# The last 256 tokens of a fused attention and feed-forward kernel: all 48 output products with tokens as stationary operand

## The chip, the cores and the metric

The kernel runs on one core of one Trainium2 chip. Its time is the device time of one execution in microseconds (us); the median of three runs before the change is 250.54 us. A second number is used below: the span of one profiled execution, from its first to its last instruction. All clock times such as "at 246.59" are us from the start of that span. The engines are called as the profile calls them: PE is the matrix engine (TensorE) and PEld its weight loads, DVE the vector engine, ACT the scalar engine, POOL the general engine, SP the engine that only issues transfers. A "q" behind an engine's name (SPq, ACTq) marks its sequencer, which waits, branches and issues transfers.

## The reference

The reference first computes a linear attention with sketched features for 4 batches of 4 heads and 1088 positions of 32 numbers. That gives x, 4352 tokens of 128 features. A feed-forward layer with a rational activation then follows:

```
h = x @ w_in                      # 4352 x 2048
P = a[0] + a[1]*h + a[2]*h*h + a[3]*h*h*h
Q = 1.0 + abs(b[0])*abs(h) + abs(b[1])*h*h
g = P / (Q + 1e-06)
out = g @ w_out                   # 4352 x 128
```

The change is in the last product, `g @ w_out`, and only for the last 256 of the 4352 tokens.

## The kernel before, in words

The kernel never forms g. With 1/Q called r, it writes g @ w_out as a sum of three products: of r, of s = h*r, and of a third array g = (h*s or h*p, times p or s), each with its own copy of w_out that has been scaled by a coefficient of P (`w_sb`, three tiles in bf16). So one block of 128 hidden features costs three matmuls, one for each of r, s and g.

The feed-forward part is cut into units of 4096 columns, where a column is one token of one block of 128 hidden features. The first unit holds 256 tokens times all 16 blocks, fourteen units hold 512 tokens times 8 blocks, and the last two, units 15 and 16, hold 256 tokens times 16 blocks. For each unit the steps are: `h` (PE, the hidden products in float32), `e` (ACT, out of PSUM into bf16), `u` (DVE, absolute value), `ln`, `ex`, `ra` (ACT, three activations that give r; `rd` is DVE's form of the third), `s`, `m`, `v`, `x` (DVE products), `pa` or `pd` (p on ACT or DVE), `G` (PE, the output products) and `st` (the store). Units other than the last take each step in halves or whole; unit 16 takes its first half whole and its second half in two quarters (`QUARTER`), so that its end is fine-grained.

The order of all steps is written out by hand in the string `ORDER` (lines 27 to 61). Each step issues its instructions on its engine's queue, and every engine works its queue in that order. Waits between engines follow from the data. Nothing is rescheduled.

For unit 16 the output products come in nine parts, `G0:16` to `G8:16` (`terms`, lines 696 to 703). Parts 0, 1, 2 are r, s, g of the first eight blocks, parts 3, 4, 5 those of the next four, parts 6, 7, 8 those of the last four: 16 blocks times three arrays are 48 products. In queue order at the end of the program they stand as G0, then 24 products of unit 15, then G7, G4, G1, G3, G6, G2, G5, G8 of unit 16.

There are two forms of such a product.

- In the usual form (`gather`, lines 744 to 749) the weights are stationary and up to 512 tokens stream past. For unit 16 it is one load of 128x128 weights and one matmul of 256 columns. The sum `outs[t0]` in PSUM has the output features on its partitions and the tokens along its columns.
- In the swapped form (`by_token`, lines 708 to 718) the data is stationary, 128 tokens of one block at a time, and the 128 output features of the weights stream past. It is two loads of 128x128 and two matmuls of 128 columns for each product. There are two sums in PSUM, one for each 128 tokens, which already have tokens on partitions and features along columns, as the output has them in DRAM.

Before the change `LATE_PARTS = (5, 8)` says that parts 5 and 8, the last eight products, are swapped. The other 40 are in the usual form. The two kinds of sum are joined by two steps. `se` (`partial`, lines 725 to 728) copies the finished sum of the 40 products, 128x256 float32, out of PSUM into an `out_sb` tile on ACT. `sx` (`turned`, lines 730 to 734) turns each 128 columns of it with a matmul against the identity and adds them into the two swapped sums; it is the last work of PE. Then `st:16` (`store`, lines 755 to 761) copies the first swapped sum out of PSUM on ACT and the second on DVE, and each engine's copy is sent to DRAM by one transfer of 64 KB, the first issued by ACT, the second by SP.

The step `fl`, just ahead of `st:16`, loads a flag into a register of every engine (line 894). The flag says whether a second, general version of the whole kernel has to run (line 942); with these inputs it has not, and each engine branches past it at the end. On SP's queue the flag's load stands between the four transfers of `st:15` (line 771, the store of unit 15) and the last transfer (line 760).

Buffers: `bank()` gives one of four PSUM banks (pool `att`), a bank is given out again when its last reader is done; `out_sb` has two buffers.

Of the kernel before, what the change touches and what calls it, by code (L numbers as in the profile page):

```python
# [11 lines left out]
FP = mybir.dt.float32  # L12
# [7 lines left out]
class Fast:  # L20
# [35 lines left out]
u1:15 ra0:15 G1:12 G2:12 h1:16 G3:13 h0:16 ln1:15 e1:16 ex1:15 e0:16 s1:14 ra1:15 pd1:14 m1:14 st:12 u0:16 x1:14 h3:16  # L56
G3:14 G1:13 ln0:16 s1:15 e3:16 ex0:16 G5:13 h2:16 G1:14 G2:13 G0:14 e2:16 pd1:15 u3:16 ra0:16 G1:15 G5:14 G3:15 G2:14
G4:14 G0:15 G0:16 m1:15 u2:16 ln3:16 x1:15 ln2:16 ex3:16 ex2:16 ra3:16 s0:16 st:14 ra2:16 pa0:16 m0:16 pa2:16 G5:15
G2:15 G4:15 s3:16 s2:16 G7:16 hi:0 G4:16 G1:16 G3:16 pa3:16 m3:16 G6:16 m2:16 x0:16 G2:16 st:15 se:16 x2:16 G5:16
x3:16 G8:16 sx:16 fl:0 st:16  # L60
    """.split()
    W_ENG = (1, 1, 0, 0, 0, 1)
    P_ON_ACT = (0, 0, 0, 0, 0, 0, 0, 0, 0, 0, 0, 0, 0, 0, 0, 0, 0, 0, 0, 0, 0, 0, 0, 0, 0, 0, 0, 0, 0, 0, 0, 0, 1, 1)
# [10 lines left out]
class General:  # L74
# [37 lines left out]
    y2:16 G3:13 pd0:15 e0:16 G4:13 s0:15 e1:16 G5:13 y3:16 pa1:14 G0:15 u0:16 m0:15 G1:15 ln1:15 G0:14 m1:14 G1:14 w0:16  # L112
    G2:14 ex1:15 x0:15 G3:14 y0:16 G2:15 v1:14 G3:15 ln0:16 s1:15 x1:14 ex0:16 pd1:15 G5:14 m1:15 G0:16 ln2:16 s0:16 G4:15
    pa0:16 x1:15 G1:16 ex2:16 m0:16 G5:15 ln3:16 s2:16 x0:16 ex3:16 m2:16 G2:16 pa2:16 st:15 s3:16 G3:16 pa3:16 G4:16
    st:14 x2:16 m3:16 G6:16 G7:16 se:16 G5:16 x3:16 sx:16 G8:16 st:16
    """.split()
    W_ENG = (1, 1, 0, 0, 0, 1)
    P_ON_ACT = (1, 1, 0, 1, 1, 0, 1, 1, 0, 1, 1, 1, 1, 0, 1, 0, 1, 0, 1, 1, 0, 1, 0, 1, 1, 1, 0, 0, 1, 1, 0, 0, 1, 1)
# [10 lines left out]
def run(  # L129
# [13 lines left out]
    nc = tc.nc  # L143
# [24 lines left out]
    mid = ctx.enter_context(tc.tile_pool(name="mid", bufs=2))  # L168
# [31 lines left out]
    for i, s_in in enumerate((S1, S2)):  # L200
# [5 lines left out]
                      in_=bass.AP(tensor=k.tensor, offset=k.offset, ap=[[S * D // 32, 128], [W, NM], [1, 4 * D]]))  # L206
    nc.sync.dma_start(out=k0[:, 0:km].rearrange("p (m x) -> p m x", m=NM - 1)[:, :, 4 * D:],
                        in_=k0_src[:, 0:km].rearrange("p (m x) -> p m x", m=NM - 1)[:, :, 4 * D:])
# [19 lines left out]
    def turn(i, cols=512):  # L228
        idle_ps = bank()
        for _ in range(plan.TURNS[i]):  # L230
            nc.tensor.matmul(idle_ps[:, :cols], lhsT=idle[:, 0:128], rhs=idle[:, :cols], start=True, stop=True)
# [17 lines left out]
    ident = consts.tile([128, 128], FP, name="ident")  # L249
# [48 lines left out]
    def bank():  # L298
        return att.tile([128, 512], FP, name="att_ps")
# [217 lines left out]
    TC = 512  # L517
    units = []
# [7 lines left out]
    live = [dict() for _ in range(NU)]  # L526
    outs, summed = {}, {}
# [64 lines left out]
    def horner(i, h):  # L592
        return 2 * i + (h > 0) in plan.HORNER

    def squared(i, h):
        return 2 * i + (h > 0) in plan.SQ
# [99 lines left out]
    def terms(i):  # L696

        per = units[i][3]
        cuts = [(0, per // 2), (per // 2, per)]
        if i in plan.QUARTER:  # L700
            cuts[1:] = [(per // 2, 3 * per // 4), (3 * per // 4, per)]
        return [[(x, y, key) for x in range(*c)] if y != 1 or not (horner(i, n) or squared(i, n)) else []
                for n, c in enumerate(cuts) for y, key in enumerate(("r", "s", "g"))]

    LATE_PARTS = (5, 8)
    by_tok = []

    def by_token(i, part):
        t0, tl, f0, per = units[i]
        tokens(i)  # L710
        count = tl // 128
        for n in range(count):
            bk, done = by_tok[n]
            for x, y, key in terms(i)[part]:
                h, c = 2 * x // per, x % (per // 2) * tl + n * 128
                nc.tensor.matmul(bk[:, :128], lhsT=part_of(i, key, h)[:, c:c + 128], rhs=w_sb[y][:, f0 + x, :],
                                 start=done[0] == 0, stop=done[0] == done[1] - 1)
                done[0] += 1

    def tokens(i):  # L720
        if not by_tok:
            total = 1 + sum(len(terms(i)[n]) for n in LATE_PARTS)
            by_tok.extend((bank(), [0, total]) for _ in range(units[i][1] // 128))

    def partial(i):
        t0, tl = units[i][:2]
        live[i]["part"] = mid.tile([128, TC], FP, name="out_sb")
        nc.scalar.copy(out=live[i]["part"][:, :tl], in_=outs[t0][:, :tl])

    def turned(i):  # L730
        tokens(i)
        for n, (bk, done) in enumerate(by_tok):
            nc.tensor.matmul(bk[:, :128], lhsT=live[i]["part"][:, n * 128:(n + 1) * 128], rhs=ident, start=done[0] == 0, stop=done[0] == done[1] - 1)
            done[0] += 1

    def gather(i, part):
        t0, tl, f0, per = units[i]
        if t0 not in outs:
            outs[t0] = bank()
            summed[t0] = [0, sum(len(z) for j in range(NU) if units[j][0] == t0 for n, z in enumerate(terms(j)) if j < NU - 1 or n not in LATE_PARTS)]  # L740
        if i == NU - 1 and part in LATE_PARTS:
            by_token(i, part)
# [40 lines left out]
    def w_part(x):  # L783
        y, f = x // 2, x % 2 * (nf // 2)
        o, t = w_sb[y][:, f:f + nf // 2], w_out_sb_f[:, f:f + nf // 2]
        if fast:
            if plan.W_ENG[x]:
                nc.scalar.activation(out=o, in_=t, func=ACT.Copy, scale=a_k[:, y:y + 1])
            else:
                nc.vector.tensor_scalar(out=o, in0=t, scalar1=a_k[:, y:y + 1], scalar2=None, op0=AX.mult)  # L790
        elif y == 2:
            (nc.scalar.copy if plan.W_ENG[x] else nc.vector.tensor_copy)(out=o, in_=t)
        elif plan.W_ENG[x]:
            nc.scalar.activation(out=o, in_=t, func=ACT.Copy, scale=a_sb[:, y:y + 1])
        else:
            nc.vector.tensor_scalar(out=o, in0=t, scalar1=a_sb[:, y:y + 1], scalar2=None, op0=AX.mult)
# [37 lines left out]
    def fitting():  # L834
        g = nc.gpsimd
        aa1, aa2, aa3 = (a_abs[:, x:x + 1] for x in (1, 2, 3))
        g.tensor_mul(out=sq, in0=ab0, in1=ab0)
        by(lim, ab1, AX.mult, 2.0 ** -10)
        by(fit, ab1, AX.is_ge, 2.0 ** -20)
        by(b4, ab1, AX.mult, 2.0)  # L840
        by(fit, ab1, AX.is_le, 2.0 ** 20, AX.mult, fit)
        by(fit, ab0, AX.is_ge, lim, AX.mult, fit)
        by(fit, b4, AX.is_ge, sq, AX.mult, fit)
        by(lim, fit, AX.mult, -1.0, AX.add, 1.0)
        by(b_fit, b_abs, AX.mult, fit, AX.add, lim)
        by(b4, b_fit[:, 1:2], AX.mult, 4.0)
        g.tensor_mul(out=sq, in0=b_fit[:, 0:1], in1=b_fit[:, 0:1])
        by(c_fit[:, 1:2], b4, AX.mult, 1.0 + 1e-6, AX.subtract, sq)
        g.tensor_copy(out=c_fit[:, 0:1], in_=b_fit[:, 0:1])
        if plan.SQ:  # L850
            for x in (2, 3):
                by(c_fit[:, x:x + 1], a_sb[:, x:x + 1], AX.is_equal, 0.0, AX.add, a_sb[:, x:x + 1])
        else:
            g.tensor_copy(out=special, in_=lim)
# [49 lines left out]
    for step in plan.ORDER:  # L904
        name, i = step.split(":")
        i = int(i)
        if name in q_does:
            getattr(blocks[i](), q_does[name])()
        elif name in k_does:
            getattr(keys[i](), k_does[name][0])(*k_does[name][1:])  # L910
        elif name == "wo":
            w_part(i)
        elif name in loads:
            fetched[name, i] = loads[name](i)
        elif name == "tn":
            turn(i)
        elif name == "ba":
            nc.scalar.activation(out=b_abs, in_=b_sb, func=ACT.Abs)
            if fast:
                if plan.SQ:  # L920
                    nc.scalar.activation(out=a_abs, in_=a_sb, func=ACT.Abs)
                fitting()
            else:
                nc.scalar.reg_load(a3_reg, a_sb[0:1, 3:4].bitcast(mybir.dt.int32))
        elif name in ("bi", "rg", "hi", "fl"):
            {"bi": factors, "rg": registers, "hi": hint, "fl": flag}[name]()
        elif name == "st":
            store(i)
        elif name == "se":
            partial(i)  # L930
        elif name == "sx":
            turned(i)
        else:
            does[name[:-1]](i, int(name[-1]))
    assert len(ready) == n_tok // 64
# [4 lines left out]
def kernel(tc, *args):  # L940
    special = run(tc, Fast, *args)
    with tc.If(special > 0, label="special"):
        run(tc, General, *args)
# [30 lines left out]
```

## Time and profile before

| what | value |
|---|---|
| median of three runs | 250.54 us |
| lowest and highest run | 250.35 us and 1419.38 us |
| the profiled execution, its own time | 253.21 us |
| its span | 251.4 us |
| granted clock of PE over the span | 0.995 |
| PE busy | 241.1 us, 96% of the span |
| DVE busy | 232.5 us, 92% |
| ACT busy | 229.4 us, 91% |

The profiled execution took 1.8 us more than its span, which lies ahead of and behind the instructions, and 2.7 us more than the median of the runs without a profiler. Differences worked out inside the span are carried over to the median; its absolute times are not.

In the rows of the timeline the columns are: start in us, length in us, engine, line of the kernel, operation, what is written and read with shapes, count of instructions merged into the row, and in brackets the idle time of the engine just before it with what ended it. The end of a matmul is modelled; its start is measured. A float32 matmul of one program line gives several rows' worth of instructions, so the two matmuls of line 733 stand as four.

### The profile page before, as it was taken

Reading aid. Unit: us, or ns where it says so; the run is one execution under the profiler, and the core shown is the slowest. Engines: PE = TensorE matmul, PEld = TensorE weight load, DVE = VectorE, ACT = ScalarE, POOL = GpSimd, SP = SyncE. Lnnn points to the kernel's source line nnn. Section 1 sums busy time; section 2 is a strip of 40 time slices with the busy share of each in tenths; the row PEclk is TensorE's granted clock in tenths of the full one; section 3 lists DMA queues with packets and bytes.
Section 4 is the critical chain, followed back from the end, with each engine's and each line's share of the span. In section 5 each row is a group of like instructions: output and inputs, shape, how many; then the busy total and the mean of one; then the engine's idle time right before and its main releaser. Section 6 shows DMA issues by size and latency. Waiting matters only on the chain. (4 is left out here: it accounts for less than half of the span.)

```text
span 251.4 us, 4115 instructions
## 1 busy us (share of the span) xinstructions
PE 241.1 (96%) x1595; PEld 135.1 (54%) x1595; DVE 232.5 (92%) x234; ACT 229.4 (91%) x220; POOL 8.0 (3%) x43
## 2 busy tenths in 40 slices
PE   6999998996999999999999999999999999999992
PEld 2778565563744544544645454544444456666781
DVE  2869799999898999999999999999999999999990
ACT  2268999999699999999999999999999999999990
POOL 4520000000000000000000000000000000000000
PEclk9999999999999999999999999999999999999997
DMA  5996346457321192062324030001000022002022
GB/s 145 240 299 223 73 125 161 152 131 118 120 78 58 47 214 56 16 146 69 81 51 125 16 106 1 0 3 28 14 0 0 0 44 42 0 0 44 0 44 46
DMA packets 29734, 19.60 MB, mean 78 GB/s; under 512 B 19344, under 2 KB 25872, under 8 KB 29712
## 3 DMA queue, kind: packets, MB, share of 16 engines
q1 hardware_dynamic: 28464, 18.92, 30.0%
q10 hardware_dynamic: 1248, 0.40, 0.9%
q8 instruction: 13, 0.21, 0.3%
q14 instruction: 9, 0.07, 0.1%
HBM read 16.16 MB, written 3.15 MB: 77 GB/s over the span
## 5 line engine op out<-in xcount | busy, mean ns | idle before, releaser
L535 PE MATMUL h_ps<-xT,w_in_sb 128*128 128x512 f32 (+1 forms) x320 | 126.5, 533 | 0.2 <-ACT hh L541 0.2
L535 PEld LDWEIGHTS h_ps<-xT,w_in_sb 128*128 128x128 f32 x320 | 58.9, 190 | 43.4 <-issue 33.4
L541 ACT CAST hh<-h_ps 128x1024 bf16<-128x1024 f32 x68 | 72.0, 1084 | 0.8 <-PE h_ps L535 0.6
L638 ACT ACTIVATE ln<-u 128x2048 f32<-128x2048 bf16 (+1 forms) x35 | 67.2, 1947 | 0.0
L747 PEld LDWEIGHTS <-w_out 128*128 128x128 bf16 x424 | 41.3, 98 | 47.0 <-issue 17.4
L643 ACT ACTIVATE r<-ln 128x2048 bf16<-128x2048 f32 x22 | 43.1, 1986 | 0.0
L668 DVE TENSOR_TENSOR s<-hh,r 128x4096 bf16<-128x4096 bf16 (+2 forms) x23 | 39.4, 1725 | 1.4 <-ACT r L649 1.2
L747 PE MATMUL att_ps<-r,w_out 128*128 128x512 bf16 (+1 forms) x160 | 34.2, 347 | 0.0
L747 PE MATMUL att_ps<-g,w_out 128*128 128x512 bf16 (+1 forms) x152 | 33.0, 351 | 0.0
L694 DVE TENSOR_TENSOR g<-g,p 128x4096 bf16<-128x4096 bf16 (+2 forms) x17 | 28.0, 1649 | 0.0
L672 DVE TENSOR_TENSOR g<-hh,s 128x4096 bf16<-128x4096 bf16 (+2 forms) x16 | 27.9, 1748 | 0.0
L655 DVE TENSOR_TENSOR r<-r 128x2048 bf16<-128x2048 bf16 x22 | 26.3, 1211 | 0.0
L643 ACT ACTIVATE ln<-ln 128x2048 f32<-128x2048 f32 (+1 forms) x13 | 24.4, 1901 | 0.0
L649 ACT ACTIVATE r<-ln 128x2048 bf16<-128x2048 f32 (+1 forms) x13 | 24.3, 1892 | 0.0
L747 PE MATMUL att_ps<-s,w_out 128*128 128x512 bf16 (+1 forms) x112 | 24.0, 349 | 0.0
L564 DVE TENSOR_SCALAR u<-hh 128x2048 uint16<-128x2048 uint16 (+2 forms) x26 | 21.9, 846 | 1.5 <-ACT hh L541 1.5
L625 DVE TENSOR_SCALAR p<-hh,a_sb 128x4096 bf16<-128x4096 bf16 (+1 forms) x17 | 21.5, 1267 | 0.0
L439 PEld LDWEIGHTS att_ps<-kvz,q_pT 128*64 128x64 f32 x288 | 9.7, 137 | 3.8 <-issue 3.3
L439 PE MATMUL att_ps<-kvz,q_pT 128*64 128x66 f32 x288 | 10.7, 224 | 1.1 <-DVE q_pT L512 0.9
L672 DVE TENSOR_TENSOR g<-hh,p 128x2048 bf16<-128x2048 bf16 (+1 forms) x7 | 11.7, 1669 | 0.0
L694 DVE TENSOR_TENSOR g<-g,s 128x2048 bf16<-128x2048 bf16 (+1 forms) x7 | 11.6, 1654 | 0.0
L375 PE MATMUL att_ps<-v_sb,k_p 128*64 128x64 f32 (+1 forms) x288 | 9.2, 223 | 2.1 <-DMA v_sb<-in_v_dram 2.1
(87 smaller groups left out, 151.7 us busy)
## 6 DMA issues: line engine op xcount, KB each, us to landing
a_all<-sk_d SPq DMA_DIRECT2D x6, 384.0 KB
b_all<-sk_d SPq DMA_DIRECT2D x12, 192.0 KB
v_sb<-in_v_dram SPq DMA_DIRECT2D x12, 144.0 KB
k_sb<-in_k_dram SPq DMA_DIRECT2D x3, 544.0 KB
q_sb<-in_q_dram SPq DMA_DIRECT2D x3, 544.0 KB
a_all<-sk_d SPq DMA_DIRECT2D x4, 320.0 KB
b_all<-sk_d SPq DMA_DIRECT2D x8, 160.0 KB
out_dram<-out_sb SPq DMA_DIRECT2D x17, 64.0 KB
```

What stands on the lines that cost most here:

```text
L535: nc.tensor.matmul(t[:, x * tl:(x + 1) * tl], lhsT=w_in_sb[:, f * 128:(f + 1) * 128], rhs=xT[:, x_at(t0):x_at(t0) + tl], start=True, stop= ...
L541: nc.scalar.copy(out=live[i]["hh"][:, part * PW:(part + 1) * PW], in_=live[i]["h", part])
L564: nc.vector.tensor_scalar(out=t[:, c].bitcast(U16), in0=live[i]["hh"][:, c].bitcast(U16), scalar1=0x7FFF, scalar2=None, op0=AX.bitwise_and)
L625: nc.vector.tensor_scalar(out=part_of(i, "p", h), in0=hh, scalar1=a3, scalar2=a2, op0=AX.mult, op1=AX.add)
L638: nc.scalar.activation(out=t, in_=live[i]["u"][:, span(h)], func=ACT.Square, scale=k_in_reg, bias=1.0)
L643: nc.scalar.activation(out=t if r_on_act(i, h) else part_of(i, "r", h), in_=t, func=ACT.Abs_reciprocal_sqrt, scale=k_sq_reg, bias=1.0)
L649: nc.scalar.activation(out=part_of(i, "r", h), in_=live[i]["ln", h], func=ACT.Square)
L655: nc.vector.tensor_mul(out=t, in0=t, in1=t)
L668: nc.vector.tensor_mul(out=part_of(i, "s", h), in0=hh, in1=part_of(i, "r", h))
L672: nc.vector.tensor_mul(out=part_of(i, "g", h), in0=hh, in1=part_of(i, "p" if horner(i, first(h)) else "s", h))
L694: nc.vector.tensor_mul(out=g, in0=g, in1=part_of(i, "s" if with_s else "p", h))
L747: nc.tensor.matmul(outs[t0][:, :tl], lhsT=w_sb[y][:, f0 + x, :], rhs=part_of(i, key, h)[:, c:c + tl], start=done[0] == 0, stop=done[0] == ...
```

## The change

`LATE_PARTS` becomes all nine parts, so all 48 products of unit 16 take the swapped form. There is no usual-form sum left for unit 16; the steps `se` and `sx`, which joined the two, are gone with their functions. Nothing else of the order is moved. The general version is changed in the same way (there G6, G7 and G5 also change places). It is not run.

```diff
@@ Fast.ORDER, its end
-... m2:16 x0:16 G2:16 st:15 se:16 x2:16 G5:16
-x3:16 G8:16 sx:16 fl:0 st:16
+... m2:16 x0:16 G2:16 st:15 x2:16 G5:16 x3:16
+G8:16 fl:0 st:16
@@
-    LATE_PARTS = (5, 8)
+    LATE_PARTS = tuple(range(9))
@@ def tokens(i):
         if not by_tok:
-            total = 1 + sum(len(terms(i)[n]) for n in LATE_PARTS)
+            total = sum(len(terms(i)[n]) for n in LATE_PARTS)
             by_tok.extend((bank(), [0, total]) for _ in range(units[i][1] // 128))
-
-    def partial(i):
-        t0, tl = units[i][:2]
-        live[i]["part"] = mid.tile([128, TC], FP, name="out_sb")
-        nc.scalar.copy(out=live[i]["part"][:, :tl], in_=outs[t0][:, :tl])
-
-    def turned(i):
-        tokens(i)
-        for n, (bk, done) in enumerate(by_tok):
-            nc.tensor.matmul(bk[:, :128], lhsT=live[i]["part"][:, n * 128:(n + 1) * 128], rhs=ident, start=done[0] == 0, stop=done[0] == done[1] - 1)
-            done[0] += 1
@@ the loop over plan.ORDER
-        elif name == "se":
-            partial(i)
-        elif name == "sx":
-            turned(i)
```

Built, the two programs issue the same instructions on DVE, SP and POOL in the same order, and on ACT the same but for the copy of line 728. On PE they are the same up to G0:16. From there 40 pairs of one weight load and one matmul of 256 columns become 80 pairs of one load and one matmul of 128 columns, and the two matmuls of line 733 are gone. The lines behind the removed code move up (716 stays; 747 becomes 736; 759 and 760 become 748 and 749; 763 and 771 become 752 and 760; 894 becomes 883; 942 becomes 927).

More of the change, by code (lines that the diff above doesn't have):

```diff
@@ L58 @@
 G4:14 G0:15 G0:16 m1:15 u2:16 ln3:16 x1:15 ln2:16 ex3:16 ex2:16 ra3:16 s0:16 st:14 ra2:16 pa0:16 m0:16 pa2:16 G5:15
[L59 to L60 removed]
+G2:15 G4:15 s3:16 s2:16 G7:16 hi:0 G4:16 G1:16 G3:16 pa3:16 m3:16 G6:16 m2:16 x0:16 G2:16 st:15 x2:16 G5:16 x3:16
+G8:16 fl:0 st:16
     """.split()
@@ L114 @@
     pa0:16 x1:15 G1:16 ex2:16 m0:16 G5:15 ln3:16 s2:16 x0:16 ex3:16 m2:16 G2:16 pa2:16 st:15 s3:16 G3:16 pa3:16 G4:16
-    st:14 x2:16 m3:16 G6:16 G7:16 se:16 G5:16 x3:16 sx:16 G8:16 st:16
+    st:14 x2:16 m3:16 G5:16 G6:16 x3:16 G7:16 G8:16 st:16
     """.split()
```

## The prediction

> **What bounds the kernel now.** I read the page's first part, then the busy time by stages of the last 15 us, then the timeline of that stretch row by row, then the rows of the sequencers at the end.
>
> ```profile
> PE 241.1 (96%) x1595; PEld 135.1 (54%) x1595; DVE 232.5 (92%) x234; ACT 229.4 (91%) x220; POOL 8.0 (3%) x43
> ```
>
> Three engines are nearly full over the span, so no share tells which one a change at the end meets. The stages do (columns: stretch, its length, then busy us and count for each engine, clock of PE, share of the DMA engines, GB/s):
>
> ```profile
> 236.30:240.70 4.40, 4.40 (x41) 3.91 (x40) 4.40 (x5) 4.40 (x6) 0.00 (x0) 1.00 0.12 19
> 241.50:243.70 2.20, 2.20 (x20) 1.95 (x20) 2.20 (x3) 2.20 (x3) 0.00 (x0) 1.00 0.23 37
> 245.40:246.50 1.10, 1.09 (x12) 0.90 (x12) 0.00 (x0) 0.00 (x0) 0.00 (x0) 1.00 0.38 61
> 246.50:251.40 4.90, 0.00 (x0) 0.00 (x0) 0.29 (x1) 0.27 (x1) 0.00 (x0) 0.73 0.17 41
> ```
>
> Up to 243.70 all three work without a gap, at full clock. From 245.40 to 246.50 PE works alone, and behind that lie 4.9 us with two short copies, the last transfers and the end of the program. The row by row timeline tells what ends what:
>
> ```profile
> 236.33 1.91 PE L747 MATMUL att_ps<-r,w_out 128*128 128x256 bf16 x16
> 240.90 0.42 PEld L747 LDWEIGHTS <-w_out 128*128 128x128 bf16 x4 [0.21 <-issue]
> 241.50 2.17 PEld L747 LDWEIGHTS <-w_out 128*128 128x128 bf16 x20 [0.18 <-issue]
> 242.56 1.22 DVE L694 TENSOR_TENSOR g<-g,p 128x2048 bf16<-128x2048 bf16 x1
> 243.70 0.44 DVE L763 STREAM_TRANSPOSE out_sb<-att_ps 128x256 f32<-128x256 f32 x1
> 243.84 0.75 PEld L747 LDWEIGHTS <-w_out 128*128 128x128 bf16 x7 [0.17 <-issue]
> 244.07 1.25 DVE L694 TENSOR_TENSOR g<-g,p 128x1024 bf16<-128x1024 bf16 x2
> 244.17 1.80 SPq L771 DMA_DIRECT2D out_dram<-out_sb  x4
> 244.77 0.45 PEld L716 LDWEIGHTS <-g 128*128 128x128 bf16 x8 [0.18 <-DVE g L694]
> 244.77 1.22 PE L716 MATMUL att_ps<-w_out,g 128*128 128x128 bf16 x16
> 244.91 0.37 ACT L728 COPY out_sb<-att_ps 128x256 f32<-128x256 f32 x1 [0.33 <-PE att_ps L747]
> 245.37 0.45 PEld L716 LDWEIGHTS <-g 128*128 128x128 bf16 x8 [0.15 <-DVE g L694]
> 245.83 0.66 PE L733 MATMUL att_ps<-ident,out_sb 128*128 128x128 f32 x4
> 246.59 0.27 ACT L759 COPY out_sb<-att_ps 128x128 f32<-128x128 f32 x1 [1.31 <-PEq L942]
> 246.59 0.29 DVE L759 COPY out_sb<-att_ps 128x128 f32<-128x128 f32 x1 [1.27 <-PEq L942]
> 246.88 0.65 ACTq L760 DMA_DIRECT2D out_dram<-out_sb  x1
> 246.91 0.64 SPq L760 DMA_DIRECT2D out_dram<-out_sb  x1
> ```
>
> From 240.90 on PE is not the bound. It stands idle five times for DVE's products (0.21, 0.18, 0.17, 0.18 and 0.15 us): at 240.90 and 241.50 it wants the two quarters of s (G7, G4), at 243.84 the first half of g (G2), at 244.77 and 245.37 the quarters of g (G5, G8). DVE makes these without a gap and ends at 244.07 + 1.25 = 245.32. So DVE sets when G8 may start, 245.37. Behind it come eight matmuls, the two against the identity (246.49), both copies (246.59, 1.31 and 1.27 us after ACT and DVE had run out), and the transfers.
>
> **The change, part by part.** *Pace of a pair.* One load and one matmul of 256 columns take (1.91 - 0.27) / 15 = 0.109 us by the row at 236.33 (0.27 is the length of one). For 128 columns there are the bursts of line 716:
>
> ```profile
> 244.77 0.62 PE L716 MATMUL att_ps<-w_out,g 128*128 128x128 bf16 x8
> L716 PE MATMUL att_ps<-w_out,g 128*128 128x128 bf16 x16 | 1.2, 221 | 0.0
> ```
>
> The first is (0.62 - 0.22) / 7 = 0.057 us; the second starts at 245.37 and is done with the sixteenth at 244.77 + 1.22 = 245.99, so (0.62 - 0.22) / 7 again. I take 0.056 to 0.057. A product in the new form costs 0.112 to 0.114 against 0.109, and 40 of them 0.1 to 0.2 us more PE work in all.
>
> *Where that falls.* G0 has 8 products, starts at 236.33 + 8 x 0.109 = 237.20 and would end 0.03 us later. The 24 products of unit 15 behind it shift by 0.03, the idle 0.21 at 240.90 takes that up, and st:15's transposing on DVE (243.70) had its sum about 3 us earlier: nothing. G7 is 8 pairs, 0.46, from 240.90 to 241.36, before the gate at 241.50. G4, G1, G3, G6 are 40 pairs, 2.28, from 241.50 to 243.78, before the gate at 243.84. G2 is 16 pairs, 0.91, to 244.75, just before the gate at 244.77. G5 and G8 stay as they are. So the extra work is hidden by the idle 0.17 and 0.18 us; if that cover were gone it would cost 0.1.
>
> *The loads now wait.* Before, the load of the weights ran ahead and only the matmul waited for data; now the load itself is the data and waits. The rows of line 716 have this already: released at 245.32, loading at 245.37, much as for G2 (DVE's g of 128x2048 ends at 242.56 + 1.22 = 243.78, PE goes at 243.84). Nothing, at most a load's length, 0.1 us, at the last gate.
>
> *The copy `se` and the turn `sx`.* ACT loses 0.37 us at 244.91, where it was idle: nothing by itself. The waits for the `out_sb` buffer (the transfers of the store of units 13 and 14) stood ahead of that copy and now stand ahead of ACT's copy of line 759; they were over before 244.91, when PE released the copy, and the copy now comes at 245.9: nothing. PE loses the turn, so its last matmul ends at 245.99 and not at 246.49. The second sum, on DVE, is copied 0.10 later as before, 246.09 to 246.38. The first sum is complete four matmuls earlier, 245.77; ACT copies it from 245.87 to 246.14. ACT's transfer is issued at 246.17, 0.71 earlier than 246.88.
>
> *SP.* The last transfer is SP's, and SP has its own queue to work off:
>
> ```profile
> L894 SPq TENSOR_LOAD <-special x1: 490/490/490, 246.0 to 246.0; - x1
> L760 SPq EVENT_SEMAPHORE  x1: 17/17/17, 246.6 to 246.6; - x1
> ```
>
> Four transfers of st:15 from 244.17, 1.80 long, to 245.97, the flag's load to 246.5, a wait of the sequencer at 246.6 that is met at once, then the transfer. Nothing of that depends on the removed steps: st:15 goes out when DVE has transposed it (243.70 + 0.44). DVE's copy will be ready at 246.38, SP not before 246.6. So SP's transfer can go out at about 246.64 and not at 246.91: 0.27 earlier, and the other 0.23 that PE gives are lost on SP. The changed kernel's next late thing is SP's queue, not PE.
>
> *PSUM.* The two swapped sums are claimed at G0 already. The sums of units 13/14 and of unit 15 are then open: four banks, four claims, and no other claim comes after it. The bank of units 11/12 was read out by DVE's transposing at 225.21:
>
> ```profile
> 225.21 0.71 DVE L763 STREAM_TRANSPOSE out_sb<-att_ps 128x512 f32<-128x512 f32 x1
> L942 SPq EVENT_SEMAPHORE  x1: 17/17/17, 249.5 to 249.5; - x1
> 248.00:249.00 1.00, 0.00 (x0) 0.00 (x0) 0.00 (x0) 0.00 (x0) 0.00 (x0) 0.87 0.54 145
> 249.00:249.70 0.70, 0.00 (x0) 0.00 (x0) 0.00 (x0) 0.00 (x0) 0.00 (x0) 0.50 0.02 4
> q8 instruction: 1, 0.02, 1.1%
> q14 instruction: 3, 0.02, 1.8%
> ```
>
> No wait, then. The other rows are for the end: SP is held until 249.5, when ACT's transfer has landed (2.6 us from its issue at 246.88), then works off the rest of its list to 251.4. The DMA engines are busy for 54% from 248 to 249 and for 2% behind that. From 246.7 on, four packets of instructions run beside the two last transfers.
>
> *Sum.* -0.27 for SP's issue, and up to 0.2 more, because the two transfers of 64 KB no longer start together and SP no longer waits for ACT's to land: I take -0.3. The span would be 251.1. Carried to the median: 250.54 - 0.3 = 250.2.
>
> **The rivals.** *A, the pairs run slower in a long stream (the one that ends slower).* Only bursts of eight pairs are seen, with a gap behind them; now 40 come without one. If p is the pace, the last matmul ends at 241.50 + 72p + 0.16 from the gate at 241.50. It passes 246.49, where the gain is gone, at p = 0.067. The far end is a load that is not hidden behind the matmul before it: the load is 98 ns long by the row below, so 98 + 56 = 154 ns.
>
> ```profile
> L716 PEld LDWEIGHTS <-g 128*128 128x128 bf16 x16 | 0.9, 98 | 0.3 <-DVE g L694 0.3
> 231.13 1.03 PE L747 MATMUL att_ps<-r,w_out 128*128 128x512 bf16 x4
> ```
>
> Then PE never waits from G0 on: 237.20 + 24 x 0.109 + 96 x 0.154 + 0.16 = 254.8, 8.3 us later than 246.49, 258.8 in all. Slower by 2% (5 us) needs p = 0.120. Against it stand both bursts, each at 57 ns with loads of 98 ns overlapping. With a load that is hidden for three quarters, 56 + 98 / 4 = 80 ns, G0 ends at 238.48, the work of unit 15 and G7 at 241.74, and 72 pairs later PE at 247.66: 1.2 us late, so 251.7.
>
> The Trainium skill has such a rule in "TensorE: Matmul & The Clock Gate", section "Back-to-back issue gap": a sustained stream of pairs of load and matmul spaces them by about 81 ns at 128 columns and 131 ns at 512, where a lone matmul's gap would be 56 and 216. By it the change would come out at about 251.8, slower, though within the 2%. The trace bears the rule out badly: at 512 columns its pairs are (1.03 - 0.38) / 3 = 217 ns apart, not 131, and at 128 columns 57 ns. No run here yet shows 128 columns in a long stream.
>
> *B, nothing moves.* SP's issue is earlier by only 0.27, and the landing may be set by something else: by the instruction packets that the branches start. If those keep their place, both transfers land as before: 250.5. For it: SP is let go at 249.5, when the DMA engines have been all but idle for 0.5 us, so a straggler sets it. Against it: the branch of SP stands behind its own transfer and so moves with it.
>
> *C, more is gained.* If the two transfers slow each other, spacing them by 0.5 us gives back 0.2 to 0.6 of the 2.6 us: 249.6 to 250.0. The Trainium skill says in "Runtime: NRT & Kernel Launch", section "Instruction fetch mechanics", that a taken branch to a page that is not held forces a fetch by DMA before the engine goes on. The four packets above agree with it; no run here shows yet what they cost.
>
> **How the numbers follow.** My forecast 0.66 (250.0 to 250.4), B 0.14, C 0.08, A 0.12: 0.09 for a pace about 80 ns, 0.03 for one of 120 ns or more. The range takes the first three, 249.6 to 250.7, and the mild part of A up to 251.2, with the spread of the runs before (250.35 and 250.54) in it; it leaves out the rest of A, less than 2 in 10. 2% is about what a measurement of this kernel can tell from no change. None of the gains comes near it: faster 0.01, slower 0.03, within 0.96.
>
> **What would show it.** Right: rows of line 716 from 241.5 on at 56 to 57 ns each, in 16 and 40 pairs; idle of PEld before G2 and G8 still there, 0.1 and 0.15; PE's last matmul near 246.0; ACT's transfer near 246.2 and SP's near 246.65, SP's behind the load of the flag. Wrong: a pace above 67 ns or PE without idle from 241.5 on (A); a new wait at G0 for a bank; SP's transfer that still goes at 246.9; the same issue times and the same end (B).

## The result, and the profile after

The changed kernel has a median of 251.87 us (251.11 to 254.02, 22 runs). The kernel before, in 22 runs that count the three shown first, has 251.05 (249.78 to 253.05, and one run of 1419.38; the 250.54 above was the median of three). The ratio is 1.0051 with a 95% interval of 1.0027 to 1.0075: 0.7 to 1.9 us slower. The ratios here and below leave out the few runs that are over 1.5% above the fastest of their kernel, and are not those of the medians (here 1.0033). That is within 2%, but it is no gain: the forecast was 0.3 us less, and its range ended at 251.2. Of the 1.7 us between the forecast's 250.2 and 251.87, 0.5 lies in its base, the median of three runs; the other 1.2 are the gain that did not come and the loss that did.

The profiled execution of the changed kernel took 251.58 us, with a span of 249.8. The span is 1.6 us shorter than that of before, although the programs are the same up to G0:16; what lies ahead of the change varies by more than the change is worth (DVE's last product ends at 245.32 in before, at 242.76 here, and between 242.4 and 244.0 in the runs below). So all positions are told from the end of DVE's last product, the second of the two rows "DVE L694 ... x2", as "+x" us. By that measure the span ends at +6.10 before and at +7.02 after: 0.92 us later.

First the page of after: PE's instructions, and the two queues that carry instructions (packets, MB).

```profile
PE 238.5 (95%) x1618; PEld 134.4 (54%) x1631; DVE 232.5 (93%) x234; ACT 228.7 (92%) x219; POOL 8.1 (3%) x43
...
q8 instruction: 14, 0.23, 0.4%
q14 instruction: 9, 0.07, 0.1%
```

PEld counts 36 loads more than before, as 40 pairs more and the four loads of the turns less must give. The matmuls should be 36 more as well and are 23, so some 13 of their records are missing.

The page of before had one packet less on q8:

```profile
q8 instruction: 13, 0.21, 0.3%
q14 instruction: 9, 0.07, 0.1%
```

A packet on q8 is 16 KB (0.23 MB / 14). The timeline of after, from G7:16 to the last transfer:

```profile
238.34 0.45 PEld L716 LDWEIGHTS <-s 128*128 128x128 bf16 x8 [0.30 <-DVE s L668]
238.34 2.12 PE L716 MATMUL att_ps<-w_out,s 128*128 128x128 bf16 x32
...
238.94 1.34 PEld L716 LDWEIGHTS <-s 128*128 128x128 bf16 x24 [0.15 <-DVE s L668]
...
240.30 1.06 PE L716 MATMUL att_ps<-w_out,r 128*128 128x128 bf16 x16
...
241.28 1.38 PEld L716 LDWEIGHTS <-g 128*128 128x128 bf16 x24
...
241.51 1.25 DVE L694 TENSOR_TENSOR g<-g,p 128x1024 bf16<-128x1024 bf16 x2
242.82 0.45 PEld L716 LDWEIGHTS <-g 128*128 128x128 bf16 x8 [0.15 <-DVE g L694]
243.26 0.27 ACT L748 COPY out_sb<-att_ps 128x128 f32<-128x128 f32 x1 [1.23 <-PE att_ps L716]
243.48 0.29 DVE L748 COPY out_sb<-att_ps 128x128 f32<-128x128 f32 x1 [0.71 <-PE att_ps L716]
243.55 0.65 ACTq L749 DMA_DIRECT2D out_dram<-out_sb  x1
244.94 0.65 SPq L749 DMA_DIRECT2D out_dram<-out_sb  x1
```

Up to the copies all is as forecast. Sixteen pairs on r take 1.06 us, (1.06 - 0.22) / 15 = 0.056 us each, in the middle of a stream of forty; PE still waits for DVE at its gates. ACT's transfer goes at +0.79, where before it went at 246.88 - 245.32 = +1.56. But DVE's copy is done at 243.77 and SP's transfer goes only at 244.94, +2.17 (positions are worked out before rounding): later than before (+1.59), and 0.85 later than the forecast's 246.64 - 245.32 = +1.32. What SP does until then, by its rows on line 760 (the store of unit 15; min, median and max of one issue in ns) and line 883 (the flag):

```profile
L760 SPq DMA_DIRECT2D out_dram<-out_sb x4: 315/454/1223, 241.6 to 243.7; - x4
```

```profile
L883 SPq TENSOR_LOAD <-special x1: 568/568/568, 244.3 to 244.3; - x1
```

```profile
L771 SPq DMA_DIRECT2D out_dram<-out_sb x4: 316/448/450, 244.2 to 245.5; - x4
```

The third fence is the store in before (line 771). Of the same four issues one now takes 1.22 us in place of 0.45. It is the third, at 242.48 in the timeline of that stretch:

```profile
242.48 1.22 SPq L760 DMA_DIRECT2D out_dram<-out_sb  x1
```

And the DMA engines of after from 242.2 to 243.4, in 40 slices of 0.03 us:

```profile
DMA  0000090024577878531000001346787863210101
GB/s 0 0 0 0 0 546 0 0 38 73 94 119 128 137 128 129 94 52 26 9 0 0 0 0 30 64 81 111 128 145 132 133 99 56 35 13 4 9 4 9
...
q8 instruction: 1, 0.02, 5.0%
```

The bytes of a packet are put down to its start: the bar of 546 is a packet of 16 KB on q8 at 242.35, and 5.0% of 16 engines for 1.2 us is 0.96 us, so it ends at 243.31. The long issue ends 0.39 behind that, at 243.70. In before no packet of q8 falls into the store.

There is a second place. From +1.0 on, in slices of 0.1 us, the DMA engines of after and of before show the two last transfers and the fetches of the branches at the program's end:

```profile
GB/s 3 0 0 0 38 129 130 31 0 83 72 69 65 163 311 338 36 174 0 0 0 0 0 0 56 256 246 57 0 82 0 5 5 10 5 10 5 0 0 0
```

```profile
GB/s 0 32 127 131 39 0 0 0 0 0 0 164 0 0 82 0 0 0 56 215 251 195 261 210 144 108 5 20 10 0 0 0 0 0 0 0 0 0 0 0
```

In after ACT's 64 KB stand in slices 13 to 16, SP's in slices 24 to 27. The bars of 174 and 164 hold the 16 KB that PE's branch fetches, those of 82 and 83 the 8 KB of another engine's. (In every version below that has the branches, such a packet of 16 KB starts 0.75 to 1.08 us behind the end of PE's branch; without the branches there is none.) Behind SP's block of data come slices of 5 to 20 GB/s: the last packets of one or two DMA engines, up to +4.7 in after and +3.9 in before. Read from the packets, SP's transfer ends at +4.66 in after and +3.87 in before, 0.79 later, of which SP's issue explains 0.58.

A transfer lands in sixteen pieces, each of which counts a semaphore up some time behind its last packet. SP's last piece lands at +4.34 before and at +5.26 after, 0.92 later, and the wait in SP's queue that it ends is met 0.02 later. First before, then after:

```profile
L942 SPq EVENT_SEMAPHORE  x1: 17/17/17, 249.7 to 249.7; - x1
```

```profile
L927 SPq EVENT_SEMAPHORE  x1: 17/17/17, 248.0 to 248.0; - x1
```

From this landing to the end of the span it is 1.76 us in both. So the landing of SP's last piece is what comes 0.92 later.

### The profile page after: what moved, and what is told of

The parts are those of the page before. It is cut to its first block, busy times and chain, and to the rows that moved or that the text cites. A ratio compares the mean times of both kernels' runs of the same rounds, so it can differ in the third digit from the quotient of the medians.

```text
span 249.8 us, 4171 instructions
## 1 busy us (share of the span) xinstructions
PE 238.5 (95%) x1618; PEld 134.4 (54%) x1631; DVE 232.5 (93%) x234; ACT 228.7 (92%) x219; POOL 8.1 (3%) x43
## 4 chain that ended last, share of the span: by engine, by line
PE 44%; ACT 26%; DVE 13%; DMA 8%; issue 5%; SPq 1%; ACTq 0%
PE h_ps L535 20%; PE att_ps L736 17%; ACT ln L638 8%; ACT hh L541 7%; ACT r L643 4%; DMA v_sb<-in_v_dram 4%; ACT r L649 3%; DVE g L694 3%; PE att_ps L716 2%; PE att_ps L375 2%; DVE s L668 2%; DVE g L672 2%; DMA k_sb<-in_k_dram 2%; ACT ln L643 1%; DVE r L655 1%
## 5 line engine op out<-in xcount | busy, mean ns | idle before, releaser
L736 PEld LDWEIGHTS <-w_out 128*128 128x128 bf16 x384 | 37.5, 98 | 45.9 <-issue 16.9
L736 PE MATMUL att_ps<-g,w_out 128*128 128x512 bf16 (+1 forms) x140 | 31.4, 355 | 0.3
L736 PE MATMUL att_ps<-r,w_out 128*128 128x512 bf16 (+1 forms) x137 | 31.2, 354 | 0.4 <-issue 0.2
L694 DVE TENSOR_TENSOR g<-g,p 128x4096 bf16<-128x4096 bf16 (+2 forms) x17 | 28.0, 1651 | 0.0
L736 PE MATMUL att_ps<-s,w_out 128*128 128x512 bf16 (+1 forms) x94 | 21.5, 361 | 0.1
L694 DVE TENSOR_TENSOR g<-g,s 128x2048 bf16<-128x2048 bf16 (+1 forms) x7 | 11.6, 1654 | 0.0
L375 PEld LDWEIGHTS att_ps<-v_sb,k_p 128*64 128x64 f32 (+1 forms) x288 | 8.9, 138 | 4.2 <-DMA v_sb<-in_v_dram 2.3
```

The source lines that it names most:

```text
L375: nc.tensor.matmul(out.rearrange("p (n d) -> p n d", d=D), lhsT=self.k_p[part][:sl, t - self.PARTS[part][0], 2 * c + a].rearrange("p i j - ...
L694: nc.vector.tensor_mul(out=g, in0=g, in1=part_of(i, "s" if with_s else "p", h))
L736: nc.tensor.matmul(outs[t0][:, :tl], lhsT=w_sb[y][:, f0 + x, :], rhs=part_of(i, key, h)[:, c:c + tl], start=done[0] == 0, stop=done[0] == ...
```

## The experiments

**The theory and the rivals.** Theory F, formed on these two traces: the swap adds 72 instructions to PE's stream (80 pairs for 40, less the two turns). PE gets its instructions in blocks, by transfers on q8. The longer stream crosses one block more, and that fetch falls into SP's issuing of unit 15's store, stretches one issue and makes SP, on whose queue the flag and the last transfer stand behind it, late. The fetches of the branches then delay the last packets. Against it, called theory S: the time is lost by the swap itself (more weight loads, the swapped store), and the fetch only coincides. The Trainium skill, "Runtime: NRT & Kernel Launch", section "Instruction fetch mechanics", has blocks of 16 KiB or 256 instructions, and calls the cost of crossing a block mostly hidden. The packets of 16 KB on q8 agree with the first; the second these runs don't bear out where the DMA issues of another engine are on the path.

The edits shift the phase of the blocks: small matmuls on zeros at the program's start, in place of some of the idle ones that stand there, add instructions and compute nothing that is used.

**After, fetch moved 80 instructions ahead.**

```diff
-    TURNS = (9, 0, 0, 0, 2, 0, 0, 0, 0)
+    TURNS = (5, 0, 0, 0, 2, 0, 0, 0, 0)
@@ def turn(i, cols=512):
+        for _ in range(44 if fast and i == 0 else 0):
+            nc.tensor.matmul(idle_ps[0:32, :32], lhsT=idle[:, 0:32], rhs=idle[:, 0:32], start=True, stop=True)
```

> The changed kernel with 80 more instructions on PE's queue in the first microseconds (44 small matmuls with their loads, 4 of the 9 idle turns less), where PE waits anyway; nothing at the end is touched. Theory F (PE's next block of instructions is fetched while SP issues the store of unit 15, and stretches that issue): the fetch, at 242.35 in the changed kernel, comes about 2 us sooner and falls into SP's pause; all four issues of that store take 0.32 to 0.46 us; SP's last transfer goes out 1.3 us after the end of DVE's last product (2.17 in the changed kernel, 1.59 before); from that product to the end of the span 5.8 us (7.02 changed, 6.09 before); ratio to the kernel before 0.998 to 1.000. Theory S (the swapped products or the earlier copy on ACT cost it by themselves): nothing changes against the changed kernel, 7.0 us and 1.005.

251.24 us, ratio to before 0.9984 (0.9956 to 1.0012), where the unshifted swap has 1.0051 (1.0027 to 1.0075): the intervals are apart. The four issues of the store, and SP's last transfer:

```profile
L762 SPq DMA_DIRECT2D out_dram<-out_sb x4: 315/448/457, 241.9 to 243.3; - x4
```

```profile
241.84 1.25 DVE L696 TENSOR_TENSOR g<-g,p 128x1024 bf16<-128x1024 bf16 x2
...
244.42 0.65 SPq L751 DMA_DIRECT2D out_dram<-out_sb  x1
```

No issue is stretched, and SP's transfer goes at 244.42, the forecast's +1.32. But the span still ends at +6.18 (expected +5.8), not before the +6.10 of the kernel before: what SP's issue gives, the last packets take, and SP's last piece lands at +4.42. The slices from +1.0 on:

```profile
GB/s 1 29 116 136 46 0 0 0 0 246 26 195 251 98 5 15 236 261 144 21 15 108 31 15 15 21 5 10 5 0 0 0 0 0 0 0 0 0 0 0
```

SP's block of data is over in slice 18 (before: 25), yet its last packets trickle to slice 28, as in before.

**Before, with the 72 instructions but without the swap.**

```diff
-    TURNS = (9, 0, 0, 0, 2, 0, 0, 0, 0)
+    TURNS = (5, 0, 0, 0, 2, 0, 0, 0, 0)
@@ def turn(i, cols=512):
+        for _ in range(40 if fast and i == 0 else 0):
+            ...
```

> The kernel before, its products as they were, with 72 more instructions on PE's queue in the first microseconds (40 small matmuls with their loads, 4 of the 9 idle turns less), so that PE's next block of instructions is fetched at about 245, while SP issues the store of unit 15. Theory F: one issue of that store takes about 1.2 us and not 0.45; SP's last transfer goes out 2.2 us after DVE's last product and not 1.59; from that product to the end of the span 6.7 to 7.0 us; ratio 1.003 to 1.004. Theory S: as the kernel before, 6.1 us and 1.000.

```profile
L773 SPq DMA_DIRECT2D out_dram<-out_sb x4: 316/450/1134, 241.9 to 244.0; - x4
```

The kernel before gets the stretched issue, 1.13 us, without any swap. SP's transfer goes at +2.00 in place of +1.59, and the span ends at +6.54 in place of +6.10. The time, 252.11 us, ratio 1.0011 (0.9982 to 1.0041), doesn't tell that 0.44 us from nothing; the trace does. All of it is less than was expected (1.2 us, +2.2, +6.7 to +7.0, 1.003 to 1.004).

**Before, with 128 instructions more (control).** As above, with 70 small matmuls and TURNS (3, ...).

> Control: the kernel before with 128 more instructions at the start (70 small matmuls with their loads, 6 of the 9 idle turns less), so that the fetch falls at about 242, between the stores of units 13/14 and 15, when SP issues nothing. Both theories: as the kernel before, 6.1 us from DVE's last product to the end, ratio 0.999 to 1.001. If the added instructions or the missing turns cost time themselves, it shows here as a ratio above 1.002 with an unchanged end.

251.09 us, ratio 0.9993 (0.9952 to 1.0033). The fetch was expected at about 242, between two stores. It falls at 236.98, into the store of units 13 and 14, and stretches one of its issues (first row, 1.17 us), with nothing urgent behind it; unit 15's store (second row) is whole, and SP's transfer goes at +1.59 as in before.

```profile
L773 SPq DMA_DIRECT2D out_dram<-out_sb x4: 315/487/1173, 236.3 to 238.4; - x4
...
L773 SPq DMA_DIRECT2D out_dram<-out_sb x4: 316/448/451, 241.3 to 242.6; - x4
```

So the added instructions by themselves cost nothing that shows here; where their fetch falls does. The span ends at +5.84, where before ends at +6.10 with SP's transfer issued at the same +1.59: so much two executions differ at the end by the landing alone.

**After, shifted, with the flag's load ahead of the store.** On SP the 0.5 us of the flag then no longer stand between the store and the last transfer.

```diff
-... G2:16 st:15 x2:16 G5:16 x3:16 G8:16 fl:0 st:16
+... G2:16 fl:0 st:15 x2:16 G5:16 x3:16 G8:16 st:16
```

> The first of these kernels, and the flag's load moved ahead of the store of unit 15 on all queues, so that it does not stand between that store and SP's last transfer. Theory F with SP's queue as the next late thing: SP's last transfer goes out as soon as DVE's copy is ready, 1.05 to 1.1 us after DVE's last product, 0.25 sooner than without the move; 5.6 us to the end; ratio 0.996 to 0.999. Theory S: 6.8 us, 1.004.

251.17 us, ratio 0.9994 (0.9967 to 1.0020): no gain. The flag is loaded on every engine, and on PE the load (0.50 us at 242.9) now stands ahead of G5 and G8:

```profile
243.45 1.05 PE L718 MATMUL att_ps<-w_out,g 128*128 128x128 bf16 x16 [0.39 <-issue]
```

PE's last matmul and both copies come 0.35 later, and SP's transfer goes at +1.38 where +1.32 was had without the move (expected +1.05 to +1.1).

**After, shifted, with the flag's load behind G0:16.** There PE has work queued and nobody waits for it.

```diff
-... G0:15 G0:16 m1:15 u2:16 ... G8:16 fl:0 st:16
+... G0:15 G0:16 fl:0 m1:15 u2:16 ... G8:16 st:16
```

> The changed kernel with the 80 early instructions, and the flag's load moved on all queues to just behind the first product group of unit 16, where PE has work queued. Against the run with the flag's load ahead of the store of unit 15, where PE's last matmul came 0.35 us later, PE's end should be back at 0.46 us after DVE's last product; ACT's transfer goes out at 0.79 and SP's at 1.05 to 1.1. From there the stragglers decide: 5.5 to 5.9 us to the end, ratio 0.997 to 0.999. If the load still holds PE up, ACT's transfer is at 1.1 again.

SP's transfer goes at +1.03, 0.3 us earlier than in any version so far, and the span ends at +5.82. The time does not follow: 251.32 us, ratio 1.0002 (0.9976 to 1.0027; expected 0.997 to 0.999).

**Both kernels without the general version.** The flag's load, the branches of all engines and what they fetch are gone; the general version is left out, and with it the step `hi`, a hint at that branch for PE, DVE, ACT and SP. The swap has the fetch shifted as above.

```diff
-    special = run(tc, Fast, *args)
-    with tc.If(special > 0, label="special"):
-        run(tc, General, *args)
+    run(tc, Fast, *args)
```

> The changed kernel with the 80 early instructions, and without the general version: no flag is loaded and no engine branches at the end, so the part of the program that other inputs would need is left out. Theory F in its second half (the branches at the end fetch instructions by DMA, and the pieces of the last two transfers that share a DMA engine with such a fetch land last and set the end): all sixteen pieces of SP's transfer land within 0.3 us of each other, none 0.5 to 1.2 us behind; without the flag's load SP's transfer goes out at 1.05 to 1.1 us after DVE's last product, when the copy is ready; its last piece lands at 3.2 to 3.4 (4.42 with the branches); 4.9 to 5.2 us to the end of the span. If the stragglers are of another kind, the last piece stays at 4.0 to 4.4 and the end at 5.9 us.

> The kernel before without the general version, in the same way: no flag, no branch, the part for other inputs left out. Theory F: SP's transfer goes out at 1.6 us after DVE's last product as before, since DVE's copy waits for the turn, its last piece lands at 3.7 to 3.9 (4.34 with the branches), 5.4 to 5.7 us to the end. Against the run with the changed products and without the general version that is 0.4 to 0.6 us more, which is then what the removed copy and turn are worth when no instruction fetch stands in the way. If the swap itself costs time, the two runs are equal or this one is shorter.

With the swap 250.23 us, ratio 0.9961 (0.9937 to 0.9985); without it 251.00, ratio 1.0005 (0.9979 to 1.0031). The intervals overlap by a little, and the means of the twelve runs are 250.11 and 251.16. Here the swap brings about 0.8 us, and the traces say the same: +4.64 against +5.43 to the end of the span, more than the 0.4 to 0.6 that were expected. SP's transfer goes at +1.03 and +1.59. The slices from +1.0 on, first with the swap, then without:

```profile
GB/s 0 31 123 130 45 0 0 0 0 0 26 225 287 180 271 256 67 0 0 0 0 0 0 0 0 0 0 0 0 0 0 0 0 0 82 0 0 0 0 0
```

```profile
GB/s 1 24 109 138 55 1 0 0 0 0 0 0 0 0 0 0 0 0 41 251 256 190 287 236 51 0 0 0 0 0 0 0 0 0 0 0 0 0 0 82
```

No trickle stands behind either block: the sixteen pieces of SP's transfer land between +2.88 and +3.06 with the swap, and between +3.67 and +3.85 without it. The kernel with the flag behind G0:16 issues both transfers at the very same times as the one with the swap here (+0.79 and +1.03), and differs from it by the flag, the hint, the branches and what they fetch:

```profile
GB/s 1 28 275 127 41 0 0 0 0 82 5 195 261 174 239 258 85 100 118 10 10 20 20 0 0 0 0 0 0 0 0 0 0 0 0 0 0 0 0 0
```

Fourteen pieces of its SP transfer land between +2.93 and +3.26, the last two at +3.62 and +4.05. Its last packet ends at +3.34 against +2.71, its span at +5.82 against +4.64, and its time is 251.32 against 250.23 us. That is the price of the branches and all that belongs to them in the changed kernel: about 1.1 us. The kernel before shows it less clearly: its end moves from +6.10 to +5.43, and its time does not tell that from nothing (1.0005). Part of it is taken back outside the span, ahead of and behind which these two executions spend 2.2 us and those with the branches 1.8 to 1.9.

**After once more, unchanged,** beside these three on one chip.

> The changed kernel once more, on the same chip and in the same rounds as the other three. Theory F: PE's block is again fetched within the store of unit 15, one of its issues takes about 1.2 us, SP's last transfer goes out at 2.1 to 2.2 us after DVE's last product, 6.8 to 7.1 us to the end, ratio 1.003 to 1.007 and so 0.4 to 0.7% above the runs with the early instructions. If the fetch falls differently in this execution and the issue is not stretched, theory F says that the end must be shorter by as much.

252.12 us, ratio 1.0036 (1.0008 to 1.0064).

```profile
L760 SPq DMA_DIRECT2D out_dram<-out_sb x4: 316/454/1225, 242.2 to 244.4; - x4
```

The stretched issue is there again, with the fetch again at -0.41 from the end of DVE's last product, and the span ends at +6.90. The flag's load on SP took 0.85 us in place of 0.57, so SP's transfer went at +2.46 (expected 2.1 to 2.2), but it landed sooner, at +5.14. On this chip the mean of the twelve runs is 252.25 us, against 251.27 for the kernel with the flag behind G0:16.

**PE held ahead of its branch.** Nine and fourteen matmuls of 512 columns on zeros behind G8, in the kernel with the flag behind G0:16; they compute nothing that is used.

```diff
-    TURNS = (5, 0, 0, 0, 2, 0, 0, 0, 0)
+    TURNS = (5, 0, 0, 0, 2, 0, 0, 0, 9)
@@
-G8:16 st:16
+G8:16 tn:8 st:16
```

> The changed kernel with the block fetch moved ahead of the store and the flag's load behind G0:16 (as in the kernel with label e7_after_early_flag0), and nine matmuls of 512 columns on zeros, 9 x 0.217 = 1.95 us, on PE behind its last product: they compute nothing that is used, and hold PE's branch and the 16 KB that it fetches back by up to 1.95 us. Theory F (the last pieces of the two transfers are late because PE's branch fetches beside them): the issues stay at +0.79 (ACT) and +1.03 (SP) from the end of DVE's last product, the fetch starts at +2.5 to +3.2 in place of +1.23, behind most of the pieces, and the last piece lands at 3.1 to 3.7 in place of 4.05; the end is at 5.2 to 5.5 in place of 5.82, unless PE's own late branch sets it. Rival (it is the small fetches of the other engines, or the branches as such): the last piece stays near 4.0 and the end at 5.8 or later.

> The same with fourteen such matmuls, 3.0 us: PE's branch and fetch come another 1.1 us later. Theory F: the last piece lands at 3.1 to 3.7 as with nine, the fetch starts at +3.6 to +4.3, behind all pieces, and what sets the end now is PE's own branch: the end at 5.8 to 6.5. Rival: the last piece near 4.0 in this one too.

251.26 us, ratio 0.9981 (0.9958 to 1.0004), with nine; 251.41, 0.9982 (0.9950 to 1.0013), with fourteen. Both expectations failed at their first step: the branch was not held. With nine, PE's rows are

```profile
L929 PEldq COMPARE_BRANCH  x1: 397/397/397, 243.8 to 243.8; - x1
```

```profile
244.17 2.11 PE L233 MATMUL att_ps<-idle 128*128 128x512 bf16 x9
```

The branch runs at 243.8 (+0.14), before the held matmuls begin; with fourteen it comes at +0.31. The fetch moved by 0.06 and 0.24 us only. The two still tell something. The issues stayed at +0.79 and +1.03, but the length of the fetch varied: it ended at +2.47 with no held matmul, at +2.75 with nine, at +2.41 with fourteen, and the last packet of SP's transfer at +3.34, +3.62 and +3.28, each time 0.87 behind it. The fetches of the other engines ended at +3.24, +3.33 and +3.25, which sets the longest apart too, but not the other two. That points at PE's fetch and does not show it. In the other versions the last packet ends 0.45 to 1.03 us behind it, and two of them have this fetch at the same place (+1.91 to +2.86) and the last packet 0.31 apart. What is shown, by the kernels without the general version, is that the branches and what they fetch delay it.

All kernels together, one execution each. "Issue" is the longest of the four of unit 15's store, "fetch" the 16 KB of PE's branch, "packet" the end of the last packet of SP's transfer, "landed" the landing of its last piece, "end" the span's; positions from the end of DVE's last product, in us, worked out before rounding.

| kernel | issue | SP's transfer | fetch | packet | landed | end | ratio to before |
|---|---|---|---|---|---|---|---|
| before | 0.45 | +1.59 | +2.17 to +3.14 | +3.87 | +4.34 | +6.10 | |
| before, 72 instructions more | 1.13 | +2.00 | +2.60 to +3.55 | +4.30 | +4.79 | +6.54 | 1.0011 |
| before, 128 more | 0.45 | +1.59 | +1.92 to +2.86 | +3.58 | +4.09 | +5.84 | 0.9993 |
| after | 1.22 | +2.17 | +2.79 to +4.21 | +4.66 | +5.26 | +7.02 | 1.0051 |
| after, again | 1.22 | +2.46 | +2.70 to +3.97 | +4.42 | +5.14 | +6.90 | 1.0036 |
| after, shifted | 0.46 | +1.32 | +1.91 to +2.86 | +3.89 | +4.42 | +6.18 | 0.9984 |
| the same, flag ahead of the store | 0.45 | +1.38 | +1.35 to +2.65 | +3.48 | +4.09 | +5.85 | 0.9994 |
| the same, flag behind G0:16 | 0.45 | +1.03 | +1.23 to +2.47 | +3.34 | +4.05 | +5.82 | 1.0002 |
| with 9 matmuls behind G8 | 0.45 | +1.03 | +1.29 to +2.75 | +3.62 | +4.28 | +6.04 | 0.9981 |
| with 14 | 0.45 | +1.03 | +1.47 to +2.41 | +3.28 | +3.83 | +5.60 | 0.9982 |
| before, no general version | 0.45 | +1.59 | none | +3.50 | +3.85 | +5.43 | 1.0005 |
| after, shifted, no general version | 0.45 | +1.03 | none | +2.71 | +3.06 | +4.64 | 0.9961 |

With the branches the end comes 1.76 to 1.77 us behind the landing of SP's last piece in every row, without them 1.58. No complete version is shown to be faster than before; the interval of the one with nine matmuls comes nearest.

## Why the prediction was wrong

**Right: the pace and its cover.** 0.056 us for a pair in a stream of forty (rival A needed 0.067). A's mild case gave 251.7 us, near the measured 251.87, but by a pace of 0.080 that did not occur; that is chance. The rule of the Trainium skill behind A, about 81 ns ("TensorE: Matmul & The Clock Gate", "Back-to-back issue gap"), is not borne out here. PE kept its waits for DVE: 0.30 and 0.15 us for s, 0.10 us for the first half of g (forecast 0.1) and 0.15 us for its last quarter, at the gates that the forecast named; no wait for a bank came.

**Right: what the removed steps free.** PE's last matmul starts at +0.46 instead of +0.90. ACT's transfer is 0.77 us earlier (forecast 0.71).

**Wrong: the step "SP".** It said of the four transfers, 1.80 long, the flag's load and the wait: "Nothing of that depends on the removed steps". SP's queue was named rightly as the next late thing, but its length was taken over from before as if it were fixed: 0.32 + 3 x 0.45 with the gaps. It depends on the instruction stream of another engine. After the change the four issues took 2.58 in place of 1.80, and SP's transfer went at +2.17, not +1.32. The kernel before with 72 idle instructions has the same stretch, and the changed kernel without it has the forecast's time for SP. So this step failed by the added instructions and where their fetch fell, and not by the products.

The trace of before could have shown it. PE's blocks came in at 202.62 and at 232.54. The busy time by stages counts what PE issued between these fetches and from the last one to the end (x of PE and PEld):

```profile
202.62:232.54 29.92, 29.92 (x142) 19.53 (x141) 29.90 (x23) 29.92 (x21) 0.00 (x0) 1.00 0.17 27
...
232.54:246.60 14.06, 13.92 (x117) 10.56 (x114) 12.79 (x16) 12.42 (x13) 0.00 (x0) 1.00 0.17 27
```

283 between two fetches, 231 from the last to the end. With 72 more it is 303, so one fetch more was due, some 20 instructions ahead of PE's end and beside the store. In after 25 rows of PE begin behind it. That another fetch was due could be told, its place less surely: earlier in the same trace there are about 185 to 300 rows between two fetches. The price stood there too: an early store of the sketch on SP, whose forty issues have a median of 0.42 us, has this row, beside a packet on q8 at 47.95:

```profile
48.12 1.17 SPq L500 DMA_DIRECT2D sk_d<-sk_sb  x1
```

Not every issue beside such a packet is stretched: those at 64.55 and 65.16 take 0.56 and 0.59 us, as others of their lines do. The prediction counted the added pairs by PE's time alone and never as instructions that have to be fetched.

**Wrong: the sum, even without that.** The sum took SP's 0.27 as 0.27 at the end, and up to 0.2 more for transfers that no longer start together and for SP's wait for ACT's. In the shifted kernel SP does go 0.27 earlier, and its last piece still lands at +4.42, where it landed at +4.34 before. That is the kind of thing that rival B named, whose chance was 0.14: the landing is set by the instruction packets. One execution doesn't settle a tenth: the kernel before and the one with 128 instructions more both issue at +1.59 and land at +4.34 and +4.09. But the five shifted kernels with the branches issue 0.21 to 0.56 earlier than that and land at +3.83 to +4.42. The argument against B, that SP's branch moves with its transfer, looked at one engine alone; the largest of the packets is PE's. The wait for ACT's transfer was worth nothing: before the change SP's own last piece lands 0.17 behind ACT's (+4.17).

Only without the branches is the sum borne out and passed: SP's transfer 0.56 earlier (the flag is gone from its queue), and 0.23 less from its issue to its last packet (1.68 against 1.91), 0.79 at the end. That these 0.23 come from the two transfers' spacing, as the sum's second term had it, no run shows by itself.

**The account.** After against before, in the traces: SP's issue 0.58 later, the landing another 0.34, 0.92 in all; the rest to the end is the same. Against the shifted swap, from which it differs in the place of the fetch, after ends 0.84 later, and 0.72 in its second execution. That is the cost of the fetch at this place. Beside SP's issue it has PE's branch in it, which takes 1.27 us here and 0.49 there, so that what the branch fetches starts at +2.79 and not at +1.91. The swap with the fetch out of the way is left at +0.08 against before, less than two executions differ by. The medians differ by 0.82, the ratio says 0.7 to 1.9; the interval is a quarter of a per cent to either side, so that the 2% which the prediction thought a measurement could tell was too coarse. Not settled: why a fetch stretches an issue of another engine, which of the branches' packets the last pieces wait behind, and how much of the 0.92 the other runs have. What lies ahead of DVE's last product, which varies by up to 2.9 us between the executions above, hides it.

## What to carry to other kernels

Count an edit's instructions as well as their time, against the number since that engine's last block fetch in the trace; an edit off the critical path can put a fetch beside transfers that are on it. Before a gain at a program's end is believed, look at what shares the DMA engines with the last transfer: here, with the transfers issued at the same times, the branches and what they fetch put the last packet 0.63 us later. To judge a change of half a per cent, compare positions from an event that both kernels have just ahead of the change, and run the unchanged kernel with the instruction count of the changed one as a control.

## What the hardware showed that was not expected

A block fetch of PE (16 KB on q8, 0.96 us) stretched a DMA issue of SP that was under way, in the stores of the output, from 0.45 us to between 1.13 and 1.22, and the issue ended 0.39 to 0.41 us behind the end of the fetch, in four executions. It is not so for every issue: with the flag ahead of the store, the 16 KB of PE's branch (+1.35 to +2.65) lie over the whole of SP's last issue (+1.38 to +2.03), and that takes 0.65 us as in the other versions. PE's branch runs ahead of queued matmuls: with 2.1 us of them still to start it had begun already. The branch itself took PE 0.39 to 0.49 us where no block fetch fell into unit 15's store, and 1.13 to 1.27 us in the three executions where one did. Loading the flag took PE's queue 0.49 to 0.50 us. Matmuls queued ahead of it went on starting (in after seven of G8, while the load ran from +0.07 to +0.56); those behind it did not (none between -0.63 and -0.03 with the flag ahead of the store).
